# Queueing the first sums of x earlier and one erf product later, where a fused retention and erf network changes to seven products a group

## The chip, the cores and the metric

The kernel runs on one core of a Trainium2 chip. Engines are named as in the profile: PE is the tensor engine, DVE is VectorE, ACT is ScalarE, POOL is GpSimd. The metric is the device time of one execution in microseconds (us). Times quoted for a kernel are medians of its runs; a profile is one of those executions, and its times count from the start of the span. The granted clock is the share of full speed at which PE was allowed to run, as the profile records it: 1.00, or 0.50 ("half clock").

## The reference

```python
# retention over batch 4, 8 heads, 768 steps, head size 64
state = gamma * state + outer(k[t], v[t])
y[t] = q[t] @ state / sqrt(64)
# bridge: x is (3072 tokens, 512)
h = x @ w_in                       # w_in 512 x 2048
g = h * erf(softplus(h))
out = g @ w_out                    # w_out 2048 x 512
```

All arithmetic is f32. The weights come in as f64, and the kernel converts them itself.

## The kernel before

Each group computes `h`, its gate (softplus, erf), the erf product `h * erf(...)`, and a projection into the output. The first 512 tokens go through four "plain" groups, with ordinary matmuls. All later tokens go through groups of seven products instead of eight, in the manner of Strassen. For these, sums of blocks of x (`x_sums`), of the two weights (`sums`) and of `g` are formed on DVE. The seven products of a group share two banks of PSUM, into which the kernel's matmuls write: products 1, 6, 7 and 4 write one, products 2, 5 and 3 the other. Product 5 begins its bank anew, so in the program it comes behind DVE's read of product 2 out of it. The retention runs chunk by chunk between the groups: scale, transpose, scores, mask, output, state.

DVE is seen to work in the order in which the program emits its instructions: in the kernel before, six weight sums (7.14 us) run in front of the sums of x, for which PE stands 3.69 us. The weight work (conversion from f64, then the weight sums) is one long stream that is emitted bit by bit: matmul code earns "pace" credits, DVE code spends them, and every whole credit emits one more step of the stream.

```python
def weights():                       # the stream; each yield is one DVE step
    ...                              # conversions of the pieces, and sums("in", 0)
    for which, n in (("in", 1), ("out", 0), ("out", 1)):
        yield from sums(which, n)    # 4 sums of 128x1024 each (line L202)

def pace(n):
    nonlocal room
    room += n
    while room >= 1:
        next(weight_steps, None)
        room -= 1

def gated(g):                        # erf product, L432
    for a in range(2):
        half = slice(a * N // 2, (a + 1) * N // 2)
        nc.vector.tensor_tensor(E[g][:, half], HS[g][:, half], E[g][:, half], op=ALU.mult)
    pace(-2.2)

def x_sums(g):                       # T1..T4, L496
    ...
    for to, a, b in ((t1, b12, b11), (t2, b22, t1), (t3, b22, b12), (t4, b21, t2)):
        nc.vector.tensor_tensor(to, a, b, op=ALU.subtract)

def hidden_part(g, p):               # one of the seven products, 16 matmuls in the profile; L513
    ...
    bank = BK[g][0 if p in (1, 6, 7, 4) else 1]     # two PSUM banks
    ...                              # matmuls into bank
    pace(1.5)
    if p == 1:   nc.scalar.copy(h["11"], flat)
    elif p == 2:                                     # the first accumulation, L526
        nc.vector.tensor_tensor(h["11"], h["11"], flat, op=ALU.add)
        pace(-0.6)
    elif p == 6: nc.scalar.copy(h["12"], flat)       # p == 6 reads T2, p == 5 reads T1
    ...

for g in range(G0, NG):              # the groups with seven products
    first = g == G0
    if first:
        x_sums(g)
        gated(g - 1)
    hidden_part(g, 1)
    hidden_part(g, 2)
    ...
    if more: T(j)                    # transposes of the next chunk, L322
    hidden_part(g, 6)
    if more: S_(j); M(j)             # scores L335, mask L347 (DVE)
    hidden_part(g, 5)
    ...
    if more: O_(j)                   # carried-state part L362, masked part L368
    hidden_part(g, 7)
    if more: U(j); A(j); ...         # state update L380
    if first: project(g - 1, 0)      # L456: first projection of the last plain group
```

## Time and profile before

The kernel before takes 762.65 us (762.43 to 762.67, 3 runs).

| what | value | how to read it |
|---|---|---|
| PE busy | 731.1 us, 96% | the bound of the kernel |
| DVE busy | 361.4 us, 48% | an average: mostly full until 171 us (151.4 us, 89%), about a third later (36%) |
| PE idle in front of product 6, first new group | 3.69 us | the place that the change aims at |
| half clock on PE there | 6.83 us | product 6 took 3.76 us for its 16 matmuls; in later groups it takes 1.8 us |

The prediction shows the lines. In them, an "x16" group is one row for 16 instructions in a row, and the first two numbers are its start and its duration.

### The profile page before, as it was taken

The page shows a single profiled execution, that of the slowest core. Times are in us where ns is not written, and L with a number is a line of the kernel's source. Part 1 is how long each engine was busy: PE and PEld are TensorE (multiplying, and loading weights), DVE is VectorE, ACT ScalarE, POOL GpSimd, SP SyncE. Part 2 cuts the span into 40 slices and gives each one's busy share as a digit, 9 for nine tenths or more (in the row PEclk, how much of TensorE's full clock was granted, in tenths as well). Part 3 has the DMA queues.
Part 4 walks back from the last instruction along what each step waited for, and adds up shares of the span by engine and source line. Part 5 has one row for each costly group of instructions (what it writes and reads, how often), then busy time and mean ns, then how long its engine had stood idle before and what let it go on. Part 6 is the DMA issues. An engine that isn't in the chain of part 4 may idle for free.

```text
span 760.7 us, 11046 instructions
## 1 busy us (share of the span) xinstructions
PE 731.1 (96%) x4896; PEld 622.6 (82%) x4896; DVE 361.4 (48%) x482; ACT 272.4 (36%) x295; POOL 31.7 (4%) x29
## 2 busy tenths in 40 slices
PE   3889999989999999999999999999999999999996
PEld 2755445448699999999999999999999999999995
DVE  5897899994324334333253153163163152153323
ACT  1334636231533423414424424424234144324430
POOL 1000001000010110010010110100000000000000
PEclk9999999998999999999999999999999999999999
DMA  9977544102120120220220220220200000000000
GB/s 230 273 182 186 153 141 123 56 0 42 56 42 9 35 70 2 41 70 2 42 71 1 42 70 1 42 62 9 43 29 1 1 28 1 1 28 1 1 28 28
DMA packets 87391, 42.66 MB, mean 56 GB/s; under 512 B 76080, under 2 KB 76080, under 8 KB 87344
## 3 DMA queue, kind: packets, MB, share of 16 engines
q1 hardware_dynamic: 86912, 41.95, 21.4%
q8 instruction: 38, 0.62, 0.4%
q14 instruction: 9, 0.07, 0.0%
q10 hardware_dynamic: 432, 0.01, 0.0%
HBM read 35.66 MB, written 6.29 MB: 55 GB/s over the span
## 4 chain that ended last, share of the span: by engine, by line
PE 90%; DVE 5%; ACT 3%; issue 2%; DMA 1%; DVEq 0%; ACTq 0%
PE hp L513 33%; PE o L570 30%; PE o L456 7%; PE hp L443 6%; PE r L335 3%; PE r L368 3%; PE r L322 2%; PE r L362 2%; PE r L380 2%; DMA w_out_sb<-in_moe_w_in_dram 1%; ACT e L412 1%; DVE am L347 1%; DVE kq L313 1%; ACT e L413 1%; ACT L412 1%
## 5 line engine op out<-in xcount | busy, mean ns | idle before, releaser
L513 PE MATMUL hp<-xs,w_in_sb 128*128 128x128 f32 x1280 | 160.6, 280 | 3.9 <-issue 3.7
L513 PEld LDWEIGHTS hp<-xs,w_in_sb 128*128 128x128 f32 x1280 | 152.0, 193 | 10.8 <-issue 7.1
L570 PE MATMUL o<-w_out_sb,h 128*128 128x256 f32 x640 | 141.6, 379 | 0.0
L432 DVE TENSOR_TENSOR e<-h,e 128x1024 f32<-128x1024 f32 x44 | 51.9, 1221 | 182.7 <-ACT e L413 182.7
L570 PEld LDWEIGHTS o<-w_out_sb,h 128*128 128x128 f32 x640 | 121.6, 190 | 16.5
L513 PE MATMUL hp<-xT,w_in_sb 128*128 128x128 f32 x960 | 113.7, 275 | 0.0
L513 PEld LDWEIGHTS hp<-xT,w_in_sb 128*128 128x128 f32 x960 | 111.9, 192 | 1.9 <-issue 1.0
L570 PE MATMUL o<-w_out_sb,e 128*128 128x256 f32 x480 | 110.3, 379 | 0.9 <-DVE e L432 0.9
L570 PEld LDWEIGHTS o<-w_out_sb,e 128*128 128x128 f32 x480 | 88.2, 190 | 11.7 <-DVE e L432 1.3
L412 ACT ACT_TABLE_LOAD x24 | 30.8, 1283 | 91.4 <-PE o L570 89.4
L443 PE MATMUL hp<-xT,w_in_sb 128*128 128x512 f32 x128 | 58.9, 608 | 0.0
L538 DVE TENSOR_TENSOR h<-h,hp 128x512 f32<-128x512 f32 x20 | 13.7, 687 | 83.3 <-PE hp L513 83.3
L533 DVE TENSOR_TENSOR h<-h,hp 128x512 f32<-128x512 f32 x20 | 13.8, 688 | 80.7 <-ACT h L531 80.7
L313 POOL TENSOR_TENSOR kq<-kq,kq_s 128x1024 f32<-128x1024 f32 x15 | 29.1, 1940 | 498.3 <-DMA kq<-in_q_dram 476.8
L443 PEld LDWEIGHTS hp<-xT,w_in_sb 128*128 128x128 f32 x128 | 24.0, 194 | 27.0 <-issue 26.7
L372 ACT COPY xT<-r 128x512 f32<-128x512 f32 x24 | 14.0, 585 | 88.9 <-PE r L368 88.9
L412 ACT ACTIVATE e<-h 128x2048 f32<-128x2048 f32 x22 | 42.0, 1911 | 0.2
L413 ACT ACTIVATE e<-e 128x2048 f32<-128x2048 f32 x22 | 42.0, 1910 | 0.2
L347 DVE TENSOR_TENSOR am<-r,causal 128x512 f32<-128x512 f32 x44 | 28.5, 684 | 21.4 <-PE r L335 20.8
L322 PE MATMUL r<-ident,kq 128*128 128x128 f32 x176 | 24.8, 284 | 14.0 <-DVE kq L313 10.8
L536 ACT COPY h<-hp 128x512 f32<-128x512 f32 x20 | 11.7, 585 | 71.9 <-PE hp L513 71.9
L322 PEld LDWEIGHTS r<-ident,kq 128*128 128x128 f32 x176 | 21.0, 147 | 15.9 <-issue 12.1
(84 smaller groups left out, 694.1 us busy)
## 6 DMA issues: line engine op xcount, KB each, us to landing
w_out_sb<-in_moe_w_out_dram SPq DMA_DIRECT2D x14, 512.0 KB, 5.1
kq<-in_k_dram SPq DMA_DIRECT2D x24, 256.0 KB, 3.5
kq<-in_q_dram SPq DMA_DIRECT2D x24, 256.0 KB, 4.2
v<-in_v_dram SPq DMA_DIRECT2D x24, 256.0 KB, 4.5
w_in_sb<-in_moe_w_in_dram SPq DMA_DIRECT2D x6, 1024.0 KB, 5.5
out_dram<-r SPq DMA_DIRECT2D x24, 256.0 KB, 2.3
w_out_sb<-in_moe_w_in_dram SPq DMA_DIRECT2D x2, 1024.0 KB, 6.9
w_in_sb<-in_moe_w_out_dram SPq DMA_DIRECT2D x2, 512.0 KB, 3.9
```

The source lines that it names most:

```text
L313: engine.tensor_tensor(KQ[j], KQ[j], by, op=ALU.mult)
L322: nc.tensor.transpose(p[:, hp, :], KQ[j][:, i, 2 * hp : 2 * hp + 2, :].rearrange("p h d -> p (h d)"), ident,)
L335: nc.tensor.matmul(pp[s][:, hp, :], KT[j][s * D : (s + 1) * D, hp, :], QT[j][s * D : (s + 1) * D, hp, :], start=True, stop=True,)
L347: nc.vector.tensor_tensor(AM[j][:, s], SC[j][s], causal[:, None, :].to_broadcast([P, HP, C]), op=ALU.mult)
L368: nc.tensor.matmul(p[s * D : (s + 1) * D, hp, :], V[j][:, 2 * hp + s, :], AM[j][:, s, hp, :], start=(not c and hp == 0), stop=True, skip_g ...
L412: nc.scalar.activation(E[g], HS[g], AF.Softplus)
L413: nc.scalar.activation(E[g], E[g], AF.Erf)
L432: nc.vector.tensor_tensor(E[g][:, half], HS[g][:, half], E[g][:, half], op=ALU.mult)
L443: nc.tensor.matmul(p, w_in_of(ft, kk), XC[0][:, kk, :], start=(kk == 0), stop=(kk == n_k - 1))
L456: nc.tensor.matmul(O[0][tt].rearrange("p (d c) -> p d c", d=2), E[g][:, u * TCH + tt * P : u * TCH + (tt + 1) * P], w_out_of(ft), start=(f ...
L513: nc.tensor.matmul(bank[:, u, :], w_in_sb[:, s, IN[a], kk, u * P : (u + 1) * P], XS[m][b][:, kk, :], start=(p in (1, 2, 5) and u == 0 and ...
L570: nc.tensor.matmul(O[m][i][:, half, :], G[g][a][:, u * P : (u + 1) * P], w_out_sb[:, s, OUT[b], u, :], start=i not in started, stop=(s == ...
```

## The change

The intent is to have T2 ready when product 6 wants it, and to get the erf product out of the way of the first accumulation. The four sums of x for the first new group are queued inside the last plain group; the erf product of that plain group is queued behind the first accumulation of the new one.

```diff
             waiting.extend(after[g][u][1])
+            if g == G0 - 1 and u == 1:
+                waiting.append((x_sums, G0))
         gate(g)
...
         first = g == G0
-        if first:
-            x_sums(g)
-            gated(g - 1)
         hidden_part(g, 1)
         hidden_part(g, 2)
+        if first:
+            gated(g - 1)
```

## The prediction

> **What bounds the kernel now.** I read the whole first and then the one place that the change touches. The summary by engine and the slices (tenths busy, granted tensor clock in tenths) say that the tensor engine (PE) is the bound:
>
> ```profile
> PE 731.1 (96%) x4896; PEld 622.6 (82%) x4896; DVE 361.4 (48%) x482; ACT 272.4 (36%) x295; POOL 31.7 (4%) x29
> ...
> PE   3889999989999999999999999999999999999996
> ...
> DVE  5897899994324334333253153163163152153323
> ...
> PEclk9999999998999999999999999999999999999999
> ```
>
> PE is full in nearly all slices of 19 us. After the start its dips are few; DVE (VectorE) is full only in the first quarter, where it converts and sums the weights beside its other work. The ninth-to-tenth slices (152 to 190 us) are where the plain groups end and the groups with seven products begin, and there the granted clock has its only dip on this row. The chain that ended last (start, duration, what) shows that place in order:
>
> ```profile
> 163.48 3.57 PE hp L513 x32
> 167.06 0.45 PE r L322 x4
> 167.51 0.02 issue
> 167.53 0.58 ACT kT L328
> 168.11 0.50 ACT qT L328
> 168.61 3.01 issue
> 171.62 3.76 PE hp L513 x16
> 175.38 1.85 PE r L335 x16
> 177.23 1.98 PE hp L513 x16
> ```
>
> Products 1 and 2 of the new group (32 matmuls) need no sums and run; eight transposes follow; then PE stands until 171.62, when product 6, the first that reads a sum of x, starts. "Issue" is only the chain's lack of a name: the timeline of DVE names it (start, duration):
>
> ```profile
> 162.45 1.22 DVE L202 TENSOR_TENSOR w_in_sb<-w_in_sb 128x1024 f32<-128x1024 f32 x1
> 163.58 7.14 DVE L202 TENSOR_TENSOR w_out_sb<-w_out_sb 128x1024 f32<-128x1024 f32 x6
> 170.64 0.42 DVE L496 TENSOR_TENSOR xs<-xT 128x256 f32<-128x256 f32 x1
> 171.09 0.42 DVE L496 TENSOR_TENSOR xs<-xT,xs 128x256 f32<-128x256 f32 x1
> 171.44 0.42 DVE L496 TENSOR_TENSOR xs<-xT 128x256 f32<-128x256 f32 x1
> 171.77 0.41 DVE L496 TENSOR_TENSOR xs<-xT,xs 128x256 f32<-128x256 f32 x1
> 172.11 2.35 DVE L432 TENSOR_TENSOR r<-h,r 128x1024 f32<-128x1024 f32 x2
> 174.49 0.69 DVE L526 TENSOR_TENSOR h<-h,hp 128x512 f32<-128x512 f32 x1
> 175.09 2.35 DVE L202 TENSOR_TENSOR w_out_sb<-w_out_sb 128x1024 f32<-128x1024 f32 x2
> 177.36 1.28 DVE L347 TENSOR_TENSOR am<-r,causal 128x512 f32<-128x512 f32 x2
> ```
>
> Product 6 needs T2, the second sum. It ends at 171.09 + 0.42 = 171.51, and PE starts 0.11 us later. There is no idle time in this list, from 162 to 178.6: DVE runs behind, with weight sums (L202) that nobody waits for yet in front of what PE waits for. PE's idle time is 3.7 us, and there is a second cost: product 6 takes 3.76 us for 16 matmuls here and 1.8 us in later groups (205.76 to 207.54), and the scores 1.85 against 1.09. Cut finely, the record of the granted clock is 0.50 from 170.11 to 176.94 us. So the place costs 3.7 us of standing, and half of the 5.3 us that PE worked at half clock (171.62 to 176.94), 2.7 us: 6.4 us in all. This is all that the change can aim at, 0.8% of 762.65 us.
>
> [...] half clock from 54.06 to 57.47 (3.41 us) and from 170.11 to 176.94 (6.83 us, two windows), and the two episodes lie 33 windows apart. [...] the window 166.70 to 170.11 with PE busy for 1.23 us (36%) led to half clock, and the window 170.11 to 173.52 with 1.90 us (56%) did not end it. [...] The trace has 416 to 422 and about 1220, so one L202 is three sums of x[...]. [...]
>
> **The change, part by part.** No instruction is added or taken away on any engine; PE, ACT, POOL and the transfers keep their order in the build of the changed kernel. Only DVE's order differs.
>
> (1) The four sums of x move from 170.64 to just before the weight step L167 that now starts at 148.75. Their cost there is what they took here, 170.64 to 172.11, 1.47 us, on a DVE that is continuously busy, so everything of DVE after them until their old place starts 1.47 us later. What waits for that? ACT's square of the last weight piece (150.27) and, behind it, the softplus and erf of the last plain group, which ended at 157.90: they slip by some 1.3 us, and ACT then has nothing to do until 165.31. The projection on PE from 149.75 reads products made at 141 to 143.4, earlier. So the move is free, and product 6 starts right behind the transposes, at 166.89 + 0.87 = 167.76.
>
> (2) The erf product (L432, two halves, 2.35 us) moves behind the first accumulation of the new group (L526). The code pays for DVE work with "pace" credits: since the erf product's debit of 2.2 now comes after the two products' credits, the weight stream is pulled further first. In the build, eight L202 on w_out, not six, stand ahead of L526. These two take 2.35 us (the row at 175.09), exactly what the erf product gave up. So L526 starts at 170.64 + 1.47 (sums, earlier) + 2.35 (two more L202) = 174.46, against 174.49 before, and the mask L347 behind the erf product at 177.36 as before. The tail of DVE's list is permuted, not shortened.
>
> **Where PE waits then.** Product 6 runs from 167.76 to 169.55, the scores to 170.64 (their inputs kT and qT are copied by 168.60). Next is product 5. It overwrites the PSUM bank of product 2, which L526 reads, so it waits for L526: 174.46 + 0.69 + 0.1 = 175.27. The old kernel hid this wait, because product 5 came only at 177.16. The new idle time is 175.27 - 170.64 = 4.6 us, longer than the 3.7 us that went, since more of the work is done before it. From there the warm steps are, by the start times of the old trace, product 5 1.89, carried-state part 0.98, masked part 1.03, product 7 1.89, state update 0.89: 6.68 us, so the projection L456 that began at 183.84 would begin at 175.27 + 6.68 = 181.95 at full clock: 1.9 us earlier. (At full clock throughout it would be 1.0 us only, since the mask of 177.36 + 0.64 holds the carried-state part to 178.05.)
>
> But 4.6 us of standing leaves some window of 3.41 us with at most 33% busy (two equal parts of 2.3 us), under the 36% that was enough to halve the clock. So the clock drops again. With c us of PE work at half clock, L456 begins at 181.95 + c/2, which breaks even at c = 3.8. If the windows lie as in this trace (boundaries at 173.52, 176.94, 180.35), the clock drops at 173.52; the window to 176.94 is busy for 1.67 us (49%, less than the 56% that was not enough), so it returns at 180.35: c = 5.1, L456 at 184.5, 0.65 us later than before. If they lie at random, and I take 75% as the return threshold (between 56 and 100), c averages 0.75 x 4.7 + 0.25 x 3.0 = 4.3, L456 at 184.1, 0.25 us later. After that PE is the bound to the end as before. I take +0.4 us: 763.0 us.
>
> **Rivals.** (a) The gap is simply removed: 6.4 us off, 756.2 us. For it: this is the intent, and product 6 really loses its wait. Against: L526 at an unchanged time. It needs L526, and the mask behind it, over 4 us ahead of my sum, and DVE has no idle time to give. (b) The gap moves and the clock stays up or returns in one short stay: 1 us off at best by the mask, 761.6. Against it stand the 36% and 56% windows. (c) The early sums delay a weight piece and the last plain group waits for it: up to 1.5 us on, 764.5. Against: the waits listed for PE have next to nothing on weight steps (0.2 us). (d) The phase of the clock windows is unlucky, c up to 6.8 us: 764.1.
>
> **Range and chances.** c between 1.9 and 6.8 us, gives -0.9 to +1.5 us; runs before spread by 0.24 us. I set 762.0 to 764.0. All of these, and (a) too at -0.8%, lie within 2%: 0.99 for that, the rest split.
>
> **What would show it.** Right: sums of x near 148.7; product 6 at about 167.8 with no wait; an idle of about 4.6 us in front of product 5, released by L526, which itself starts near 174.5 behind eight weight sums; a stretch of half clock there of one or two windows; L456 at 183 to 185. Wrong if L526 starts by 172, if the clock stays at 1.00 through that idle time, or if PE waits before 163 us where it did not.

The 416 to 422 ns are the median times of one f32 sum of 128x256 (L496), the 1220 ns the time of one of 128x1024 (L202). A "window" is 3.41 us: the half clock lasted once or twice that in the kernel before (3.41 and 6.83 us), and I count on from its edges in steps of that length. The 75% was an estimate of mine, between the two windows of the kernel before in which PE was busy for 56% and for 100%: half clock went on after the first and ended after the second. That windows may lie anywhere against the kernel's work is an assumption.

## The result

The changed kernel takes 763.34 us (762.64 to 764.48, 6 runs), against 762.54 us (761.15 to 762.91, 6 runs) of the kernel before. The ratio is 1.0016, with a 95% interval of 1.0003 to 1.0029. In these rounds the change made the kernel 0.8 us slower, with an interval of 0.2 to 2.2 us: it did not help, and the loss is less than the runs of one kernel differ (below).

The timeline of PE of the changed kernel, around the first new group (start, duration, engine, line, operation; in brackets the idle time in front and what ended it):

```profile
164.56 3.73 PE L513 MATMUL hp<-xT,w_in_sb 128*128 128x128 f32 x32
168.13 1.04 PE L322 MATMUL r<-ident,kq 128*128 128x128 f32 x8
169.01 1.95 PE L513 MATMUL hp<-xs,w_in_sb 128*128 128x128 f32 x16
170.89 1.16 PE L335 MATMUL r<-qT,kT 64*128 64x128 f32 x16
176.68 3.78 PE L513 MATMUL hp<-xs,w_in_sb 128*128 128x128 f32 x16 [4.63 <-DVE h L526]
180.25 1.88 PE L362 MATMUL r<-qT,state 128*128 128x128 f32 x8
182.06 1.09 PE L368 MATMUL r<-am,v 128*64 128x128 f32 x16
183.09 2.05 PE L513 MATMUL hp<-xs,w_in_sb 128*128 128x128 f32 x16
184.97 1.06 PE L380 MATMUL r<-v,kq 128*128 128x128 f32 x8
185.87 3.60 PE L456 MATMUL o<-w_out_sb,r 128*128 128x512 f32 x8
```

Product 6 (169.01) now follows the transposes with no wait and at full speed (1.95 us for 16 matmuls). The next product, 5 (176.68), waits 4.63 us instead, and it is product 5 that now takes 3.78 us for 16 matmuls. The timeline of DVE says what was in front of L526, the accumulation that product 5 waits for:

```profile
149.81 0.42 DVE L496 TENSOR_TENSOR xs<-xT 128x256 f32<-128x256 f32 x1
...
160.69 1.22 DVE L179 SCALAR_TENSOR_TENSOR w_out_sb<-w_out_sb 128x1024 f32<-128x1024 f32 x1 [0.47 <-DVE w_out_sb L177]
161.83 4.75 DVE L202 TENSOR_TENSOR w_in_sb<-w_in_sb 128x1024 f32<-128x1024 f32 x4
166.50 9.41 DVE L202 TENSOR_TENSOR w_out_sb<-w_out_sb 128x1024 f32<-128x1024 f32 x8
175.94 0.69 DVE L526 TENSOR_TENSOR h<-h,hp 128x512 f32<-128x512 f32 x1
176.54 2.35 DVE L432 TENSOR_TENSOR r<-h,r 128x1024 f32<-128x1024 f32 x2
178.81 1.28 DVE L347 TENSOR_TENSOR am<-r,causal 128x512 f32<-128x512 f32 x2
```

The sums of x are early. Eight weight sums, not six, are in front of L526, and the erf product is behind it. The windows view of the changed kernel (stretch, its length, busy time of PE, PEld, DVE, ACT and POOL, then the granted clock, the DMA share and GB/s) shows three windows of 3.41 us there, counted from the edges of the half clock (175.14 and 181.96):

```profile
171.72:175.14 3.42, 0.33 (x6) 0.14 (x4) 3.39 (x4) 0.00 (x0) 0.00 (x0) 1.00 0.00 0
175.14:178.55 3.41, 1.87 (x9) 1.87 (x9) 3.38 (x4) 0.00 (x0) 0.00 (x0) 0.50 0.00 0
178.55:181.96 3.41, 3.41 (x17) 3.32 (x16) 1.54 (x3) 0.00 (x0) 0.00 (x0) 0.50 0.00 0
```

The clock halves after the window with PE busy for 0.33 us (10%), stays halved through one that is 55% busy and through the full one, and is back at 1.00 after that. DVE is busy through the first two (3.39 and 3.38 us): it was never waiting.

To compare profiles, I count from the start of product 1 (the 32 matmuls at 163.32 before and 164.56 after), because the first 40 us differ from one execution to the next. The changed kernel's profile has 1.12 us of unnamed waiting of PE at 35.06 us. The profile of "sums_early" below has the early sums too, lacks this wait and starts product 1 at 163.01, while "before_hold8", which has nothing of the change, has a like wait (1.40 us in front of 36.13) and starts product 1 at 164.58. So this shift is not the change's. Counted so, the projection L456 begins 20.52 us after product 1 before and 21.31 us after it in the changed kernel: 0.79 us later. That is also the difference of the two medians (0.80 us), though with one profile of each kernel so close a match is in part luck.

### The profile page after: what moved, and what is told of

Same layout as the page of the kernel before. It is cut to its first block, busy times and chain, and to the rows that moved or that the text cites. A ratio compares the mean times of both kernels' runs of the same rounds, so it can differ in the third digit from the quotient of the medians.

```text
span 762.8 us, 11046 instructions
## 1 busy us (share of the span) xinstructions
PE 731.6 (96%) x4896; PEld 623.2 (82%) x4896; DVE 361.2 (47%) x482; ACT 272.7 (36%) x295; POOL 32.0 (4%) x29
## 4 chain that ended last, share of the span: by engine, by line
PE 78%; DVE 15%; ACT 2%; issue 2%; DMA 1%; SPq 0%; DVEq 0%; ACTq 0%
PE hp L513 33%; PE o L570 30%; PE r L368 3%; PE r L335 3%; PE r L322 2%; PE r L362 2%; DVE w_out_sb L177 2%; PE o L456 2%; PE r L380 2%; DVE w_out_sb L175 2%; DVE w_in_sb L167 1%; PE hp L443 1%; DVE w_out_sb L202 1%; DVE w_in_sb L202 1%; DVE e L432 1%
## 5 line engine op out<-in xcount | busy, mean ns | idle before, releaser
L513 PE MATMUL hp<-xs,w_in_sb 128*128 128x128 f32 x1280 | 160.5, 280 | 4.8 <-DVE h L526 4.8
L513 PEld LDWEIGHTS hp<-xs,w_in_sb 128*128 128x128 f32 x1280 | 152.0, 193 | 11.6 <-DVE h L526 5.2
L432 DVE TENSOR_TENSOR e<-h,e 128x1024 f32<-128x1024 f32 x44 | 51.9, 1221 | 182.7 <-ACT e L413 182.7
L513 PE MATMUL hp<-xT,w_in_sb 128*128 128x128 f32 x960 | 113.7, 275 | 0.0
L513 PEld LDWEIGHTS hp<-xT,w_in_sb 128*128 128x128 f32 x960 | 112.0, 192 | 1.9 <-issue 1.0
L347 DVE TENSOR_TENSOR am<-r,causal 128x512 f32<-128x512 f32 x44 | 28.5, 685 | 21.4 <-PE r L335 20.8
```

The costliest lines, as they stand in the source:

```text
L347: nc.vector.tensor_tensor(AM[j][:, s], SC[j][s], causal[:, None, :].to_broadcast([P, HP, C]), op=ALU.mult)
L513: nc.tensor.matmul(bank[:, u, :], w_in_sb[:, s, IN[a], kk, u * P : (u + 1) * P], XS[m][b][:, kk, :], start=(p in (1, 2, 5) and u == 0 and ...
```

## The experiments

My theory was that the queue of DVE sets the end of this stretch, and that the change only permutes that queue. In the kernels whose names begin with "hold" (and "before_hold8") the code has three more lines, so L513, L526, L432 and L347 are L516, L529, L435 and L350 there. All nine kernels gave right results. This table is read from the profiles and runs; "wait 6", "wait 5" and "wait c" are PE's idle times in front of product 6, product 5 and the carried-state part, all in us.

| kernel | wait 6 | wait 5 | wait c | product 1 to projection | half clock there | median | ratio to before (95%) |
|---|---|---|---|---|---|---|---|
| before | 3.69 | - | - | 20.52 | 6.83 | 762.54 | 1 |
| changed | - | 4.63 | - | 21.31 | 6.83 | 763.34 | 1.0016 (1.0003 to 1.0029) |
| sums_early | - | 4.62 | - | 21.12 | 6.82, two windows | 762.55 | 1.0008 (0.9992 to 1.0023) |
| erf_late | 3.68 | - | - | 20.57 | 6.82, two windows | 762.59 | 1.0010 (0.9997 to 1.0022) |
| warm | - | 1.05 | 0.82 | 19.87 | none | 761.69 | 0.9998 (0.9986 to 1.0011) |
| hold2 | - | 2.38 | - | 18.18 | 3.41, one window | 759.51 | 0.9962 (0.9948 to 0.9976) |
| hold4 | - | - | 0.82 | 15.22 | none | 757.01 | 0.9929 (0.9917 to 0.9942) |
| hold8 | - | - | - | 14.10 | none | 755.87 | 0.9918 (0.9902 to 0.9933) |
| before_hold8 | - | - | - | 14.10 | none | 756.01 | 0.9921 (0.9909 to 0.9933) |

**sums_early: the first half of the change alone.** The erf product goes back to its old place.

```diff
+        if first:
+            gated(g - 1)
         hidden_part(g, 1)
         hidden_part(g, 2)
-        if first:
-            gated(g - 1)
```

> Only the sums of x move into the last plain group; the erf product keeps its old place in front of the new group's products. My theory: product 6 starts with no wait, but six weight sums and the erf product still stand ahead of the first accumulation, so it ends some 11.9 us after the start of product 1 as before, PE waits about 4.6 us in front of product 5, at half clock after it: the same as the whole change, 0 to +1.5 us against the kernel before (ratio 1.000 to 1.002). Rival, that the late erf product spoils a gain which the early sums give: this run is 3 us or more faster than before (ratio below 0.996).

As the theory had it: product 6 waits for nothing, product 5 waits 4.62 us, the ratio is 1.0008. DVE's list shows the trade plainly:

```profile
164.94 7.14 DVE L202 TENSOR_TENSOR w_out_sb<-w_out_sb 128x1024 f32<-128x1024 f32 x6
171.99 2.35 DVE L432 TENSOR_TENSOR r<-h,r 128x1024 f32<-128x1024 f32 x2
174.38 0.69 DVE L526 TENSOR_TENSOR h<-h,hp 128x512 f32<-128x512 f32 x1
```

Six weight sums and the erf product, or eight weight sums: L526 starts 11.37 us after product 1 here, and 11.38 us after it in the changed kernel. The projection comes 0.19 us sooner than there, which is half of the difference in PE's work at half clock (4.91 us, 175.12 to 180.03, against 5.28 us). The rival (the erf product spoils a gain) falls: its ratio, below 0.996, lies outside the interval.

**erf_late: the second half alone.** The sums of x stay where they were (the edit is shown against the changed kernel).

```diff
-            if g == G0 - 1 and u == 1:
-                waiting.append((x_sums, G0))
...
         first = g == G0
+        if first:
+            x_sums(g)
```

> Only the erf product moves behind the first accumulation; the sums of x stay at the start of the new group. My theory: product 6 waits for the second sum of x as before (about 3.7 us idle), product 5 then finds the first accumulation done, and the time is that of the kernel before within 0.5 us (ratio 0.9993 to 1.0007). Rival, that the late erf product costs by itself by delaying the projection of the last plain group: slower than before by 1 us or more.

The wait in front of product 6 is 3.68 us, as before, and the projection begins at 20.57 us, within 0.05 us of before. The ratio of 1.0010 lies above what I expected, and its interval (0.9997 to 1.0022) includes both 1 and the rival's 1 us (1.0013). So the runs alone do not decide; by the profile, one execution, a later erf product costs nothing by itself. Its reader, the projection, comes only at 20 us.

**warm: filling the new gap with repeated matmuls.** The scores of the one chunk are written five times over, each time with the same values, so that PE does not stand.

```diff
-    def ret_scores(j):
+    def ret_scores(j, again=0):
         pp = SC[j] = [ret_psum() for _ in range(2)]
-        for hp in range(HP):
+        for hp in list(range(HP)) * (1 + again):
...
-            S_(j)
+            S_(j, 4 if first else 0)
             M(j)
```

> The changed kernel with the score matmuls of the one chunk in the gap written five times over (the same result each time, 64 more matmuls of some 68 ns, 4.4 us), so that PE is busy in the time in which it would wait. Right result expected. My theory: the granted clock stays at 1.00 there, product 5 starts at the same 12.0 us after product 1's start, the mask of DVE holds the carried-state part a little, and the projection that follows begins 1.5 to 2 us earlier than in the changed kernel: 1.8 us faster than it, 1.0 us faster than before (ratio 0.9987). Rival, that the half clock costs nothing that a wait does not cost anyway: as the changed kernel (ratio 1.001) or slower, for 4.4 us of added work.

With 64 more matmuls the projection comes 1.44 us sooner than in the changed kernel (19.87 against 21.31 us), and the clock stays at 1.00. That is what the half clock cost in the changed kernel, less the new wait for the mask; DVE's queue still sets the start of product 5 (12.11 us after product 1, 12.12 in the changed kernel). Timeline of PE in this kernel:

```profile
169.54 4.74 PE L335 MATMUL r<-qT,kT 64*128 64x128 f32 x80
175.32 2.05 PE L513 MATMUL hp<-xs,w_in_sb 128*128 128x128 f32 x16 [1.05 <-DVE h L526]
178.19 1.16 PE L362 MATMUL r<-qT,state 128*128 128x128 f32 x8 [0.82 <-DVE am L347]
```

Product 5 is at full speed and ends early, so the mask, behind the erf product, holds the carried-state part for 0.82 us, as the prediction had said of a kernel at full clock. I expected 1.0 us off the kernel before; the profile gives 0.65 us and the runs give a ratio (0.9998) from which no gain can be read. The 80 score matmuls took some 59 ns each, not 68, so that PE still stood for 1.05 us, and product 5 started 0.1 us later than I had it (12.11 for 12.0).

**hold8: the weight sums of w_out held back.** Eight steps of the weight stream wait until the mask has been emitted. Nobody reads these sums before the second new group.

```diff
         for which, n in (("in", 1), ("out", 0), ("out", 1)):
-            yield from sums(which, n)
+            for _ in sums(which, n):
+                tail[0] += 1
+                yield
+
+    tail, held = [0], [12 - 8]
...
-        while room >= 1:
+        while room >= 1 and not (held and tail[0] >= held[0]):
...
             S_(j)
             M(j)
+            if first:
+                held.clear()
```

> The changed kernel with the eight weight sums of w_out, which nobody reads before the second of the new groups, held back until the mask of the first has been issued. My theory, that DVE's queue ahead of the first accumulation is all that keeps PE: no wait in front of product 6 or product 5, granted clock 1.00 throughout, and the projection 6.5 us earlier than before: ratio 0.9915 (756 us). Rival, that another wait takes its place (the weight sums pushed behind, then the second accumulation or a later product): 0.995 or more.

The ratio is 0.9918 (0.9902 to 0.9933): the expected 0.9915 lies in the interval, the rival's 0.995 does not. The waits are gone, and the queue shows why (timeline of DVE):

```profile
167.02 0.69 DVE L529 TENSOR_TENSOR h<-h,hp 128x512 f32<-128x512 f32 x1 [1.84 <-PE hp L516]
167.63 2.35 DVE L435 TENSOR_TENSOR r<-h,r 128x1024 f32<-128x1024 f32 x2
170.70 1.29 DVE L350 TENSOR_TENSOR am<-r,causal 128x512 f32<-128x512 f32 x2 [0.71 <-PE r L338]
171.90 9.41 DVE L202 TENSOR_TENSOR w_out_sb<-w_out_sb 128x1024 f32<-128x1024 f32 x8
181.23 0.68 DVE L536 TENSOR_TENSOR h<-h,hp 128x512 f32<-128x512 f32 x1
```

Now DVE waits for PE (1.84 us in front of the accumulation), and the weight sums run in time that was idle. They do push the next accumulation a little (it follows at once), but PE does not stand for it.

**hold2 and hold4: how much of the queue matters.** The same edit with 2 and 4 in place of 8.

> The changed kernel with two of the eight weight sums of w_out held back until after the mask, so that six stand ahead of the first accumulation, as many as in the kernel before. My theory: the first accumulation starts 2.35 us sooner, 9.0 us after product 1's start instead of 11.4; PE waits about 2.3 us in front of product 5 instead of 4.6, and may or may not fall to half clock there; the projection begins 17.4 (full clock) to 19.5 us (half clock for one window) after product 1, against 20.5 before and 21.3 in the changed kernel: ratio 0.996 to 0.999. Rival, that the wait is set by something other than the queue ahead of the accumulation: unchanged, 1.001.

> As hold2 with four held back: the first accumulation starts 6.7 us after product 1 and is done before the scores end, so product 5 waits for nothing; now the mask, behind the erf product, is last, and PE waits about 1.0 us in front of the carried-state part; clock 1.00; projection 15.1 us after product 1, 5.4 us earlier than before: ratio 0.993. Rival: proportional to the number held, so half of what eight gave, ratio 0.996.

With two held, six weight sums are in front of the first accumulation, as in the kernel before, but the sums of x are early and the erf product is behind it: product 5 waits 2.38 us and the clock still halves for one window (3.41 us). With four held, product 5 waits for nothing, and the mask is last, by 0.82 us. Both are close to the expected figures (18.18 us for 17.4 to 19.5; 15.22 for 15.1), and the gains are not proportional: the first two sums give 3.1 us, the next two 3.0 us, the last four 1.1 us. Here a queue in front of a reader was worth its length only until another reader was last.

**before_hold8: the kernel before with the same hold and nothing of the change.**

> The kernel before, its order of sums of x and erf product untouched, with the eight weight sums of w_out held back until the mask. My theory: the second sum of x is done some 2.5 us before product 6 needs it, the accumulation before product 5 needs it, and nothing of the change is needed: the time of the changed kernel with eight held, ratio 0.992, projection 14.1 us after product 1. Rival, that the changed order has a worth of its own once the queue is short: 1 us or more slower than that kernel (ratio above 0.9932).

The projection comes at 14.10 us, as in hold8, and the ratio is 0.9921. Once the weight sums are out of the way, neither half of the change has a worth of its own that these runs can show.

**hold8_mask and hold8_mask_state: the same remedy at the other place.** PE waits 3.2 us at some 50 us, also behind weight steps. The mask of chunk 4 is queued right after its scores; in the second kernel the addition to the running state is too.

```diff
-            ([(S_, 4), (T, 5)], [(M, 4)]),
+            ([(S_, 4), (M, 4), (T, 5)], []),
-            ([(O_, 4), (U, 4), (S_, 5)], [(A, 4), (M, 5), (K_, 6)]),
+            ([(O_, 4), (U, 4), (A, 4), (S_, 5)], [(M, 5), (K_, 6)]),   # second kernel only
```

> The changed kernel with eight held back, and the same remedy in the one other place where PE waits over 3 us and the clock falls: the mask of chunk 4 is queued right after its scores, ahead of two weight steps (2.5 us), so that the transposes of chunk 5 get their bank sooner. My theory: the wait of 3.2 us there shrinks below 1 us and the half clock of 3.4 us goes, 2.5 + 1.7 = 4.2 us on top of the 6.2 of hold8: ratio 0.986 (751.5 us). Rival, that DVE is the bound in the first 60 us and PE then waits for the delayed weight steps: no better than hold8, 0.991.

This missed. The ratio is 0.9916 (0.9902 to 0.9930), 755.30 us: no better than hold8. The wait of 3.2 us shrank to 0.78 us as expected, but the next one grew (timeline of PE):

```profile
51.38 1.25 PE L325 MATMUL r<-ident,kq 128*128 128x128 f32 x8 [0.78 <-DVE am L350]
...
61.54 1.95 PE L338 MATMUL r<-qT,kT 64*128 64x128 f32 x14 [2.05 <-DVE state L400]
```

PE arrived sooner, waited 2.05 us for a state addition queued behind weight steps, where it had waited 0.62 us, and the clock halved there (61.65 to 65.06 us). So the rival's figure came true, though not by its road: PE waited for an addition behind the weight steps, not for the weight steps themselves.

> As hold8_mask, with the addition of chunk 4's state to the running state also queued right behind its matmuls, ahead of three weight steps. In hold8_mask the gain of the mask was given back 8 us later: PE waited 2.05 us for that addition and the clock fell to half for some 3.4 us there. My theory: this wait shrinks below 0.8 us and the half clock goes, 1.3 + 1.6 = about 3 us faster than hold8_mask, ratio 0.988 (753 us at 762.4 before). Rival, that DVE is the bound in the first 70 us and each place freed opens the next: no better than hold8_mask, 0.9916 within 0.001.

With the state addition moved too, that wait is 0.62 us and the mean granted clock of the profiled run is 1.0. It takes 752.23 us (752.11 to 752.34, 4 runs), ratio 0.9863 (0.9833 to 0.9893), which includes the 0.988 that I expected and leaves out the rival's 0.9916. This is the fastest kernel, some 10 us under the kernel before in the same rounds (762.58 us).

## Why the prediction was right

The result, 763.34 us, lies within the range of 762.0 to 764.0, near the 763.0 given, and by the predicted road: the sums came early, product 6 lost its wait, product 5 waited for L526 behind eight weight sums, and the clock fell. That the number fits so well is in part luck: two of the six runs (764.39 and 764.48) lie outside the range, which is also a little narrower than the -0.9 to +1.5 us that it was drawn from.

- **The sums of x are free to move.** Nearly. Product 6 starts 4.45 us after product 1 (4.44 by the prediction's times). But a conversion step behind them, L179, stood 0.47 us, where such a step starts 0.10 us behind its forerunner otherwise. All eight kernels with early sums show it (0.47 to 0.48 us), the three without do not. The trace names only DVE's own step in front of it, so its cause stays open. L526 came 11.38 us after product 1, against 11.17 in the kernel before and 11.14 by the prediction's times: 0.2 us of slowdown that I had not in the sum, and the extra stand is long enough to account for it. One sign of being wrong was a wait of PE before 163 us where there was none; the profile has one, at 35.06 us, long before the moved sums, and a kernel without the change has it too (see the result).
- **Two more weight sums take the place of the erf product.** Shown by the order, by sums_early against the changed kernel, and from the other side by hold2.
- **The wait moves to product 5, 4.6 us.** 4.63 us, released by L526.
- **The clock drops again, for some 5.1 us of work.** 5.28 us (176.68 to 181.96), and warm shows by experiment that it cost 1.44 us net of the mask's hold.
- **The sum.** Predicted +0.65 us with the windows of that trace, +0.25 us for windows at random, and +0.4 us as the figure between; measured +0.79 us in the profiles and +0.80 us in the medians. The excess over 0.65 us is mostly the later start of product 5 (12.12 us after product 1, for 11.95). The average of 4.3 us at half clock was a little high: worked through with the prediction's own 36% (measured) and 75% (estimated), it comes to 4.1 us, which is worth 0.1 us.
- **Rival (a), the gap simply removed.** Not what the change did, but its figure for the prize, 6.4 us, stands: hold8 took 6.42 us out of the stretch (20.52 - 14.10), by shortening the queue.

One supporting figure was wrong: that runs of the kernel before spread by 0.24 us. That came from three runs. In 29 later runs it spread from 759.69 to 763.97 us, mostly in step with the granted clock. The three that had a mean clock of 1.000 took 759.69 to 760.16; thirteen had 0.993 and took 761.77 to 762.77; five had 0.991 and took 763.46 to 763.97; the other eight lay between in clock and took 761.03 to 762.77. A mean of 1.000 leaves no room for a stretch of half clock (the two in the profile, 10.24 us together, make 0.993), so in those three runs the wait of 3.7 us must have escaped it; that is inferred, as they left no trace to look at. None of the six runs of the changed kernel did: their clock was 0.991 to 0.993. I had reckoned with this luck for the changed kernel only, not for the one that it is compared with. The spread of the kernel before, 4.3 us, is wider than the whole range, so that the difference of two medians fell inside it owes something to luck.

## What to carry to other kernels

In this kernel an engine (PE, 3.69 us) waited for one instruction of another (DVE) that had fallen behind and worked in the emitted order. Moving that instruction ahead moved the wait to the next reader of the same queue (4.63 us); only moving work without an early reader behind the readers took the wait away (hold8: no wait there). So look at everything in the queue, ask of each entry who reads it first and when, and follow the freed engine to its next wait before counting a gain. A scheme that emits filler work by credit reacts to the edit too: compare the emitted orders, not the source.

## What else the traces and runs show

- Windows of 3.41 us with PE busy for 0.33 us (changed kernel), 1.03 (hold2), 1.23 (kernel before) and 1.36 (from 58.24 us in hold8_mask, 40%) were followed by half clock, and windows of 1.87 us (changed kernel) and 1.90 (kernel before), 55 and 56%, did not end it. A window of 3.12 us (91%, from 53.38 us in hold8) did end it. So waits of 2.38 us (hold2) and 2.05 us (hold8_mask), well under a window, had half clock after them. In warm PE stood 1.05 us and then 0.82 us, with product 5 (2.05 us) between the two, and the clock stayed at 1.00.
- For comparing kernels it matters that the same kernel took 759.69 to 763.97 us at mean clocks of 1.000 to 0.991, five times the effect of the change.
- An f32 sum of 128x1024 (L202) took about 1220 ns in these traces. The cause of the extra 0.37 us in front of one L179 in the kernels with early sums is open.
